# Linear attention ahead of two expert layers: a new order in the first rounds, and work moved in the last ones

## The chip, the cores and the metric

One core of one Trainium2 chip. The metric is the device time in microseconds (us) of one execution of the program. The kernel before took 772.84 us (median of 3 runs, 772.15 to 774.85).

## What is computed

Three layers, one behind the other, all in float32. The first is a linear attention with decay, over 4 batches, 8 heads, 768 steps and a head dimension of 48:

```python
for t in range(S):
    cur = einsum('bhd,bhe->bhde', u * k[t], v[t])
    y[t] = einsum('bhd,bhde->bhe', r[t], state + cur)
    state = w * state + einsum('bhd,bhe->bhde', k[t], v[t])
```

Its 3072 rows of 384 values go through a mixture of 8 experts (each token through the one with the largest logit, `relu(x @ w1[e]) @ w2[e]`, scaled by its gate) and then through a dense layer, `h = x @ w_in; (h - tanh(h)) @ w_out`.

## The kernel before, in words

**Tiles and rounds.** The sequence is cut into 6 chunks of 128 steps (C = 6); a tile is one chunk of one batch (B = 4), so there are 24 tiles, `seq[n]`, and the loop at L755 runs one round n for each, plus one more. Within a tile the recurrence is written as matrix products: the decays become tables of powers of w (`tables`, L284), with which r and k are scaled; the scores of all pairs of steps are masked to earlier ones, the diagonal holds the term with u, and the product with v gives the output. What earlier chunks left comes in through a state for each batch. Two buffers of scores (PSUM tags A0 and A1, one for the even and one for the odd heads) serve all tiles.

**The operations of a round**, by the engine that they run on:
- SP issues the loads, all from one queue in the order of the program: `load(n + 3)` (L233) brings n (r, k, v by token, 576 KB) and t (r, k transposed, 384 KB) of a tile into one of 5 buffers; `xout_g` writes finished rows to `xd`; `w_load` (L66) brings expert weights.
- POOL (GpSimd) computes `side`: rk = r*k, rku = rk*u, and `side_kh` (L349): kh = k*KT, for tile n + 2. `sw` (in `state_add`) scales the old state.
- DVE (VectorE): `diag_sum` (L354, dt) sums rku by head; `scale` (L324) multiplies r and k of tile n + 1 by the tables, k from round 3 on by PRK, a copy in SBUF; `mask` (L375) copies the scores of earlier steps into am; `state_add` (L393). Later rounds add the gate (`gate`), the ranks of the tokens (`rank_of`, `rank_in`), `head_end` (L492) and the subtraction of `w_split` (L79), which cuts a float32 weight in two parts.
- ACT (ScalarE): `diag` (L359) writes the 8 diagonals into am, one operation for each head; the copies of the output to y; xs (in `xout_g`, L573); the first half of `w_split`.
- PE (TensorE): `scores` (L366), `outp` (L408; the part on the old state is L418, the part with am L423), `state_mm` (L381, L390), `logits` (L447, L452), `xout_t` (L562; transposes of the output for `xout_g`). `keep_warm` (L586) issues products that nobody reads.

**Order.** Each engine works through its instructions in the order in which the program issues them; this block is scheduled by hand (`manual_schedule`), so the order of the calls is the order on each engine. Across engines semaphores order what depends on each other, buffers included. In round n the calls stand as: `load(n+3)`, `diag_sum(n+1)`, `scale(n+1)`, `logits`, `xout_t` (in rounds 5, 9, 13, ... it stands behind outp), `outp(n-1)`, `state_mm(n)`, `xout_g`, `diag(n+1)`, `scores(n)`, a second `xout_t` and `xout_g` where a round has two, `mask(n)`, `state_add(n)`, `side(n+2)`, `side_kh(n+2)`, and the gate and rank steps of a chunk that is complete. XOUT (L754) says which tiles leave in which of the last rounds; in the others it is tile n - 7. LOADS (L751) and SPLITS (L752) say in which round a half of a weight block is loaded and a quarter of it split.

**One PSUM bank.** `x_bank` (L433) hands the bank with tag X to `logits` and to `xout_t` in turn; from round 23 on a second one, K, takes every other turn:

```python
def x_bank(name):
    turns.append(name)
    tag = "K" if "both" in st and len(turns) % 2 else "X"
    return ps1.tile([P, HP, P], F32, tag=tag, name=name)
```

**Round 0 and the ends.** Ahead of the loop `in_range` (L267) tests the decays (each must lie between 3/4 and 4/3; for one that does not, a slow path runs, by the flag of `range_flag`, L279) and puts 1 in place of those that fail. In round 0 `k_rows` (L309) transposes the table of k on PE and copies it to KT on ACT, which kh needs. `gate_rows` (L247, round 0) clears pkg on DVE and loads the gate's columns in two transfers on SP's queue; `gate_cols` (L260, round 1) lays them out on POOL. Behind round 22's rank steps `head_gather` (L597) fetches, by index, the first rows of the first expert from `xd`, for which it needs idxh (an end of `idx_mm` in round 21) and the rows of tiles 0 to 15. After the loop PE transposes them (L610), and the experts' products and then the dense layer follow.

## Time and profile before

| | us |
|---|---|
| median of 3 runs | 772.84 |
| lowest, highest | 772.15, 774.85 |
| the profiled execution, its own time | 772.78 |
| its span, first to last instruction | 771.1 |
| PE busy | 755.7 (98% of the span) |
| DVE busy | 639.2 (83%) |
| ACT busy | 509.1 (66%) |
| POOL busy | 430.9 (56%) |

The profile is of one execution. Times of its rows count from the start of the span. Attention lies in the first 120 us or so, the experts up to about 375, the dense layer behind. "L372" is a line of the kernel before. PE is the engine of the matrix products, DVE VectorE, ACT ScalarE, POOL GpSimd, SP the queue that issues most transfers. "Idle before" is the time that an engine stood still ahead of an instruction, and the name behind the arrow is what ended it. The mean granted TensorE clock over the span was 0.996 of full speed.

### The profile page before, as it was taken

Reading aid. Unit: us, or ns where it says so; the run is one execution under the profiler, and the core shown is the slowest. Engines: PE = TensorE matmul, PEld = TensorE weight load, DVE = VectorE, ACT = ScalarE, POOL = GpSimd, SP = SyncE. Lnnn points to the kernel's source line nnn. Section 1 sums busy time; section 2 is a strip of 40 time slices with the busy share of each in tenths; the row PEclk is TensorE's granted clock in tenths of the full one; section 3 lists DMA queues with packets and bytes.
Section 4 is the critical chain, followed back from the end, with each engine's and each line's share of the span. In section 5 each row is a group of like instructions: output and inputs, shape, how many; then the busy total and the mean of one; then the engine's idle time right before and its main releaser. Section 6 shows DMA issues by size and latency. Waiting matters only on the chain.

```text
span 771.1 us, 14624 instructions
## 1 busy us (share of the span) xinstructions
PE 755.7 (98%) x5200; PEld 684.6 (89%) x5200; DVE 639.2 (83%) x1155; ACT 509.1 (66%) x1091; POOL 430.9 (56%) x435
## 2 busy tenths in 40 slices
PE   8899989999999999999999999999999999999997
PEld 7688868998999999999898998989989989899887
DVE  7899996788899888964898888888888888888893
ACT  6788885464454445554887766776777677677881
POOL 6989952385877876765355353443534344343433
PEclk9999999999999999999999999999999999999999
DMA  8999945466999899974000010000001000000101
GB/s 238 261 291 290 318 128 167 145 189 201 256 230 271 223 305 286 250 198 144 1 1 0 1 42 1 0 21 21 1 1 42 1 1 24 18 1 1 41 1 42
DMA packets 34656, 89.67 MB, mean 116 GB/s; under 512 B 5499, under 2 KB 12704, under 8 KB 34578
## 3 DMA queue, kind: packets, MB, share of 16 engines
q1 hardware_dynamic: 30384, 78.68, 34.8%
q0 software_dynamic: 4192, 9.99, 4.6%
q8 instruction: 43, 0.70, 0.4%
q14 instruction: 35, 0.29, 0.1%
q10 hardware_dynamic: 2, 0.00, 0.0%
HBM read 72.92 MB, written 15.74 MB: 115 GB/s over the span
## 4 chain that ended last, share of the span: by engine, by line
PE 51%; issue 2%; ACT 1%; POOL 1%; POOLq 0%
PE h L1346 25%; PE o L1394 24%; PE y L1119 1%; PE hps L1094 1%; POOL out_dram L1407 0%; PE o L1346 0%; POOL g L1383 0%; POOLq L1453 0%; POOL xb L1383 0%; ACT s L1354 0%; ACT mk L1356 0%; POOLq L1507 0%; ACT xb L1382 0%; ACT z L1350 0%; ACT t L1352 0%
## 5 line engine op out<-in xcount | busy, mean ns | idle before, releaser
L1383 POOL TENSOR_TENSOR g<-t,g 128x512 fp32r<-128x512 f32 x93 | 120.3, 1294 | 178.6 <-ACT g L1382 128.5
L1346 PE MATMUL h<-xb,ring 128*128 128x512 f32 x855 | 213.6, 395 | 0.0
L1394 PE MATMUL o<-ring,g 128*128 128x384 f32 x1116 | 209.3, 336 | 0.0
L1394 PEld LDWEIGHTS o<-ring,g 128*128 128x128 f32 x1116 | 196.1, 188 | 8.2
L1346 PEld LDWEIGHTS h<-xb,ring 128*128 128x128 f32 x855 | 159.7, 188 | 30.5
L85 POOL TENSOR_TENSOR ring<-stg,ring 128x384 fp32r<-128x384 f32 x102 | 105.3, 1053 | 53.8 <-ACT ring L84 42.4
L1350 ACT ACTIVATE z<-h 128x512 f32<-128x512 f32 x95 | 56.9, 599 | 95.2 <-PE h L1346 95.2
L1119 PE MATMUL y<-h,ring 128*128 128x256 f32 (+7 forms) x576 | 114.2, 342 | 0.6 <-DVE h L1098 0.6
L1094 PE MATMUL hps<-xt,ring 128*128 128x472 f32 (+6 forms) x504 | 105.6, 353 | 0.1
L1119 PEld LDWEIGHTS y<-h,ring 128*128 128x128 f32 x576 | 101.3, 188 | 4.1 <-DVE h L1098 1.0
L1362 DVE TENSOR_TENSOR t<-t,h 128x512 f32<-128x512 f32 x95 | 65.1, 685 | 41.3 <-ACT t L1352 40.9
L1094 PEld LDWEIGHTS hps<-xt,ring 128*128 128x128 f32 x504 | 90.6, 188 | 3.7 <-DVEq L1233 0.4
L1367 DVE COPY_PREDICATED t<-mk,h 128x512 f32<-128x512 uint32 x95 | 71.4, 751 | 10.1 <-DVE h L1365 0.5
L84 ACT CAST ring<-stg 128x384 fp32r<-128x384 f32 x152 | 70.2, 512 | 9.5 <-DMA stg<-in_wp_dram 8.9
L1364 DVE SCALAR_TENSOR_TENSOR h<-s,h 128x512 f32<-128x512 f32 x95 | 66.2, 697 | 10.6 <-ACT g L1382 0.9
L1097 ACT ACTIVATE h<-hps 128x256 fp32r<-128x256 f32 (+7 forms) x64 | 32.1, 501 | 63.8 <-PE hps L1094 61.8
L1354 ACT ACTIVATE s<-z,gb 128x512 f32<-128x512 f32 x96 | 69.6, 725 | 0.0
L1356 ACT ACTIVATE mk<-z,gt 128x512 f32<-128x512 f32 x96 | 69.3, 721 | 0.0
L1365 DVE SCALAR_TENSOR_TENSOR h<-z,h 128x512 f32<-128x512 f32 x95 | 66.1, 696 | 3.3
L1363 DVE TENSOR_TENSOR h<-h,z 128x512 f32<-128x512 f32 x95 | 65.9, 693 | 0.0
L1382 ACT CAST g<-t 128x512 fp32r<-128x512 f32 x93 | 57.6, 619 | 9.7 <-DVE t L1367 7.8
L363 ACT ACTIVATE am<-ident,dt 128x128 f32<-128x128 f32 x192 | 58.6, 392 | 3.8 <-DVE dt L356 3.8
(254 smaller groups left out, 1039.6 us busy)
## 6 DMA issues: line engine op xcount, KB each, us to landing
stg<-in_wp_dram SPq DMA_DIRECT2D x64, 384.0 KB, 4.9
n<-in_rkv_dram SPq DMA_DIRECT2D x24, 576.0 KB, 6.0
d<-in_wp_dram SPq DMA_DIRECT2D x32, 384.0 KB, 5.8
t<-in_rk_t_dram SPq DMA_DIRECT2D x24, 384.0 KB, 7.1
wdec<-dcf SPq DMA_DIRECT2D x32, 192.0 KB, 5.3
xd<-xs SPq DMA_DIRECT2D x24, 192.0 KB, 3.9
stg<-wdec SPq DMA_DIRECT2D x12, 384.0 KB, 4.3
wl<-wdec SPq DMA_DIRECT2D x2, 768.0 KB, 6.0
```

The lines of the kernel that those rows point to most:

```text
L84: nc.scalar.copy(out=dst[:, 0, sl], in_=of)
L85: eng.tensor_tensor(out=dst[:, 1, sl], in0=of, in1=dst[:, 0, sl].bitcast(F32), op=ALU.subtract)
L1094: nc.tensor.matmul(ps, lhsT=wf(a, kk), rhs=xt[e][b][:, kk, :], start=(n == 0), stop=(n == 8))
L1119: nc.tensor.matmul(yps[d], lhsT=wf(a)[:, d * P:(d + 1) * P], rhs=h2[:, b, :], start=(f == 0 and n == 0), stop=(f == CH1 - 1 and n == 2))
L1346: nc.tensor.matmul(ps, lhsT=wf(a, kk), rhs=xb[j][:, b, kk, :], start=(n == 0), stop=(n == 8))
L1354: nc.scalar.activation(out=s, in_=z, func=ACTF.Square, scale=G_K ** 0.5, bias=gb)
L1356: nc.scalar.activation(out=mk, in_=z, func=ACTF.Relu, scale=-1.0, bias=gt2)
L1364: nc.vector.scalar_tensor_tensor(out=ps, in0=s, scalar=G_K * G_D, in1=ps, op0=ALU.add, op1=ALU.mult)
L1365: nc.vector.scalar_tensor_tensor(out=ps, in0=z, scalar=G_A, in1=ps, op0=ALU.subtract, op1=ALU.mult)
L1367: nc.vector.copy_predicated(out=t, mask=mk.bitcast(U32), data=ps)
L1383: nc.gpsimd.tensor_tensor(out=g[:, 1, :], in0=ww, in1=g[:, 0, :].bitcast(F32), op=ALU.subtract)
L1394: nc.tensor.matmul(ops[q], lhsT=gg[i][:, b, q * P:(q + 1) * P], rhs=wf(a), start=(f == 0 and n == 0), stop=(f == CH2 - 1 and n == 2))
```

## The change

Seven edits. (1) The decays are bounded to 3/4 and 4/3 by one operation straight into the table of powers, and whether any was changed is found out in round 1 (`unchanged`). (2) keep_warm(14) ahead of the loop becomes keep_warm(8). (3) Round 0 begins with tile 0's scores, k_rows, the KT copy, the second half of its diagonals, its mask and its kh, ahead of diag_sum(1) and scale(1). (4) In rounds 1 to 4 scores(n), mask(n) and five of the eight diagonals of tile n + 1 stand ahead of outp(n-1); outp is cut in two functions for that, the part on the old state and the rest. (5) side_kh does nothing for the tiles of the last chunk (20 to 23), whose state nobody uses. (6) Tiles 12 to 15 leave two by two in rounds 19 and 20 in place of one each in 19 and 20 and two in 21; splits and one load move by a round or two, and two of the splits subtract on POOL in place of DVE. (7) head_end moves from round 19 to round 21, gate_cols from round 1 to round 3.

```diff
--- before.py
+++ after.py
@@ -199,7 +199,6 @@
     orow = ap_.tile([1, P], F32, name="orow")
     pkg = ap_.tile([P, 2, E * HP], F32, name="pkg")
     wcol, ucol = pkt[:, 0:HP], pkt[:, HP:2 * HP]
-    wsafe = ap_.tile([PT, HP], F32, name="wsafe")
     flag = ap_.tile([1, 1], I32, name="flag")
     wgp = ap_.tile([P, HP, 32], F32, name="wgp")
     sel = ap_.tile([P, E], F32, name="sel")
@@ -265,15 +264,13 @@
                                   in_=pkg[rows].rearrange("p q (i g e) -> p g q i e", g=2, e=E)[:, g])
 
     def in_range():
-
-        sq = ap_.tile([PT, HP], F32, name="sq")
-        nc.vector.tensor_mul(out=sq, in0=wcol, in1=wcol)
-        hi = ap_.tile([PT, HP], F32, name="hi")
-        nc.vector.tensor_single_scalar(out=hi, in_=sq, scalar=16.0 / 9.0, op=ALU.is_le)
+        nc.vector.memset(pw[:, :, 0:1], 1.0)
+        nc.vector.tensor_scalar(out=pw[:, :, 1:2], in0=wcol.unsqueeze(2), scalar1=0.75, scalar2=4.0 / 3.0,
+                                op0=ALU.max, op1=ALU.min)
+
+    def unchanged():
         ok = ap_.tile([PT, HP], F32, name="ok")
-        nc.vector.scalar_tensor_tensor(out=ok, in0=sq, scalar=9.0 / 16.0, in1=hi, op0=ALU.is_ge, op1=ALU.mult)
-        nc.vector.memset(wsafe, 1.0)
-        nc.vector.copy_predicated(out=wsafe, mask=ok.bitcast(U32), data=wcol)
+        nc.vector.tensor_tensor(out=ok, in0=wcol.unsqueeze(2), in1=pw[:, :, 1:2], op=ALU.is_equal)
         return ok
 
     def range_flag(ok):
@@ -283,9 +280,10 @@
 
     def tables():
 
-        for t, base, n in ((pw, wsafe.unsqueeze(2), 16), (pq, pw[:, :, 16:17], 8)):
-            nc.vector.memset(t[:, :, 0:1], 1.0)
-            nc.vector.tensor_copy(out=t[:, :, 1:2], in_=base)
+        for t, base, n in ((pw, None, 16), (pq, pw[:, :, 16:17], 8)):
+            if base is not None:
+                nc.vector.memset(t[:, :, 0:1], 1.0)
+                nc.vector.tensor_copy(out=t[:, :, 1:2], in_=base)
             m = 1
             while m < n:
                 nc.vector.tensor_tensor(out=t[:, :, m + 1:2 * m + 1], in0=t[:, :, 1:m + 1],
@@ -310,6 +308,10 @@
         kps = sm[:, 64:64 + HP * PT].rearrange("p (j t) -> p j t", t=PT)
         for j in range(HP):
             nc.tensor.transpose(kps[:, j, :], KD3[:, j, :], ident[0:PT, 0:PT])
+        st["kps"] = kps
+
+    def k_rows_end():
+        kps = st.pop("kps")
         nc.scalar.copy(out=KT.rearrange("p (j q) d -> p j (q d)", q=2), in_=kps[:, :, R0:R0 + 2 * D])
 
     def zero_pad(i, eng):
@@ -347,6 +349,8 @@
         side_rku(n)
 
     def side_kh(n):
+        if seq[n][0] == C - 1:
+            return
         kh = kh_b[n % 3]
         nc.gpsimd.tensor_tensor(out=kh[:, R0:].rearrange("p (h d) -> p h d", d=D), in0=n_b[n % NB][:, 1], in1=KT, op=ALU.mult)
         st["kh", n] = kh
@@ -356,12 +360,13 @@
         nc.vector.tensor_reduce(out=dt, in_=st.pop(("rku", n)), axis=AX.X, op=ALU.add)
         st["dt", n] = dt
 
-    def diag(n):
-        dt = st.pop(("dt", n))
-        am = at3.tile([P, 2, HP, P], F32, tag="am", name="am")
-        for h in range(H):
-            nc.scalar.activation(out=am[:, h % 2, h // 2, :], in_=ident, func=ACTF.Copy, scale=dt[:, h:h + 1])
-        st["am", n] = am
+    def diag(n, part=range(H)):
+        if 0 in part:
+            st["am", n] = at3.tile([P, 2, HP, P], F32, tag="am", name="am")
+        dt, am = st["dt", n], st["am", n]
+        for q, j in (divmod(k, HP) for k in part):
+            h = 2 * j + q
+            nc.scalar.activation(out=am[:, q, j, :], in_=ident, func=ACTF.Copy, scale=dt[:, h:h + 1])
 
     def scores(n):
         t = t_b[n % NB]
@@ -405,10 +410,8 @@
         state_mm(n)
         state_add(n)
 
-    def outp(n):
+    def outp_state(n):
         c, b = seq[n]
-        am = st.pop(("am", n))
-
         if c > 0:
             for i in range(2):
                 for g in range(2):
@@ -417,6 +420,10 @@
                         j, p0 = 2 * i + g, 64 * g
                         nc.tensor.matmul(Yp[q][p0:p0 + D, i, :], lhsT=Sc[c % 2][b][rows, j, :],
                                          rhs=t_b[n % NB][rows, 0, j, :], start=(i == 0), stop=False)
+
+    def outp(n):
+        c, b = seq[n]
+        am = st.pop(("am", n))
         for q in range(2):
             for j in range(HP):
                 i, p0 = j // 2, 64 * (j % 2)
@@ -724,12 +731,12 @@
         zero_pad(1, nc.scalar)
         keep_warm(6)
         u_rows()
-        keep_warm(14)
+        keep_warm(8)
         for i in range(3, NB):
             zero_pad(i, nc.scalar)
         consts()
         side_rk(0)
-        ok = in_range()
+        in_range()
         tables()
         NN = len(seq)
 
@@ -742,16 +749,16 @@
         side_rku(0)
         scale(0)
         diag_sum(0)
-        diag(0)
+        diag(0, range(HP))
         k_table()
         side(1)
         nc.gpsimd.memset(cum[0], 0.0)
-        LAG = 7
+        LAG, AHEAD = 7, B + 1
         L = C - 1
-        LOADS = {5: (0, 0), 9: (0, 1), 13: (1, 0), 15: (1, 1), 17: (2, 0), 20: (2, 1), NN - 1: (3, 0)}
-        SPLITS = {8: (0, 0), 12: (0, 1), 16: (0, 2), 18: (0, 3), **{NN - 3 + k: (1, k) for k in range(3)}}
+        LOADS = {5: (0, 0), 9: (0, 1), 13: (1, 0), 15: (1, 1), 17: (2, 0), 21: (2, 1), NN - 1: (3, 0)}
+        SPLITS = {9: (0, 0), 13: (0, 1), 17: (0, 2), 20: (0, 3, nc.gpsimd), 21: (1, 0, nc.gpsimd), 22: (1, 1), 23: (1, 2)}
         LATER = {0: ((3, 0), (3, 1)), 1: ((2, 2), (2, 3)), 2: ((3, 2), (3, 3))}
-        XOUT = {NN - 3: (NN - 10, NN - 9), NN - 2: (), NN - 1: (NN - 8, NN - 7), NN: ()}
+        XOUT = {NN - 5: (NN - 12, NN - 11), NN - 4: (NN - 10, NN - 9), NN - 3: (), NN - 2: (), NN - 1: (NN - 8, NN - 7), NN: ()}
         for n in range(NN + 1):
             if n == NN:
                 w_split(1, 3)
@@ -761,6 +768,13 @@
                 load(n + 3)
             if n in LOADS:
                 w_load(*LOADS[n])
+            if n == 0:
+                scores(0)
+                k_rows()
+                k_rows_end()
+                diag(0, range(HP, H))
+                mask(0)
+                side_kh(0)
             if n + 1 < NN:
                 diag_sum(n + 1)
                 scale(n + 1)
@@ -772,7 +786,13 @@
                 st["both"] = True
             if xs_of and not with_logits:
                 xout_t(xs_of[0])
-            if 1 <= n <= NN:
+            if n:
+                outp_state(n - 1)
+            if 0 < n < AHEAD:
+                scores(n)
+                mask(n)
+                diag(n + 1, range(5))
+            if n:
                 outp(n - 1)
                 at_step(n, 6, rank_row)
             if n > 1 and n < NN:
@@ -782,15 +802,16 @@
             if xs_of:
                 xout_g(xs_of[0])
             if 0 < n < NN - 1:
-                diag(n + 1)
+                diag(n + 1, range(5 if n < AHEAD else 0, H))
             if n < NN:
-                scores(n)
+                if n >= AHEAD:
+                    scores(n)
                 for m in xs_of[1:]:
                     xout_t(m)
                     xout_g(m)
-                mask(n)
+                if n >= AHEAD:
+                    mask(n)
                 if n == 0:
-                    k_rows()
                     diag(1)
                 elif n == 1:
                     state(0)
@@ -800,7 +821,6 @@
             if n + 2 < NN:
                 side(n + 2)
                 if n == 0:
-                    side_kh(0)
                     side_kh(1)
                 side_kh(n + 2)
             at_step(n, 3, logits2)
@@ -811,7 +831,7 @@
             at_step(n, 4, rank_mm)
             at_step(n, 4, rank_of)
             at_step(n, 5, rank_in)
-            if n == H0 * B + 3:
+            if n == NN - 3:
                 head_end()
             if n == NN - 2:
                 head_gather()
@@ -820,10 +840,11 @@
                 gate_rows()
             if n == 1:
                 scale_rows()
-                gate_cols()
+                ok = unchanged()
                 nc.vector.tensor_reduce(out=nok, in_=ok, axis=AX.X, op=ALU.add)
                 nc.vector.memset(one, 1.0)
             if n == 3:
+                gate_cols()
                 range_flag(ok)
                 nc.vector.tensor_copy(out=e8p, in_=e8)
                 nc.vector.tensor_copy(out=thp, in_=thr)
```

## Rows read from the trace of the kernel before

**Rows 1.** Page, engines; then stretches: us, busy us by engine, PE clock, DMA share, GB/s

```profile
PE 755.7 (98%) x5200; PEld 684.6 (89%) x5200; DVE 639.2 (83%) x1155; ACT 509.1 (66%) x1091; POOL 430.9 (56%) x435
...
28.00:30.00 2.00, 2.00 (x31) 1.81 (x29) 1.93 (x10) 0.77 (x3) 2.00 (x3) 0.56 0.95 250
30.00:32.00 2.00, 2.00 (x23) 1.80 (x19) 0.87 (x2) 2.00 (x8) 1.92 (x3) 0.59 1.06 256
...
80.00:90.00 10.00, 9.87 (x180) 7.49 (x176) 9.86 (x23) 9.18 (x29) 8.71 (x10) 1.00 1.02 304
...
140.00:160.00 20.00, 20.00 (x170) 19.88 (x170) 15.03 (x45) 10.86 (x28) 11.52 (x11) 1.00 0.58 179
```

**Rows 2.** Waits of POOL, 0 to 30 us: total us, times, longest

```profile
POOL rk L336 <- DMA n<-in_rkv_dram: 4.7, 3, 1.8
```

**Rows 3.** Timeline, 2 to 16 us: start us, us, engine, line, operation, idle before

```profile
2.88 0.14 DVE L270 TENSOR_TENSOR sq<-pkt 112x4 f32<-112x4 f32 x1
...
3.88 0.81 DVE L291 TENSOR_TENSOR pw<-pw 112x4 f32<-112x4 f32 x4
...
5.96 5.86 PE L589 MATMUL yh<-ident 128*128 128x128 f32 x28
...
13.49 0.48 ACT L313 COPY KT<-sm 128x384 f32<-128x384 f32 x1 [1.45 <-PE sm L312]
13.50 1.34 DVE L377 COPY_PREDICATED am<-mlt,A 128x512 f32<-128x512 uint32 x2
...
14.92 0.81 SPq L250 DMA_DIRECT2D pkg<-in_pk_dram  x2
```

**Rows 4.** Timeline, rounds 1 to 4

```profile
21.88 0.47 POOL L264 COPY wgp<-pkg 64x32 f32<-64x32 f32 x2
...
27.86 1.71 PE L423 MATMUL yh<-am,n 128*48 128x128 f32 x16 [1.70 <-DVE am L377]
...
30.29 1.80 PE L372 MATMUL A<-t 64*128 64x128 f32 x16
...
32.19 1.36 DVE L377 COPY_PREDICATED am<-mlt,A 128x512 f32<-128x512 uint32 x2 [1.32 <-PE A L372]
```

**Rows 5.** Timeline, rounds 18 to 21

```profile
95.96 0.81 DVE L85 TENSOR_TENSOR ring<-stg,ring 128x384 fp32r<-128x384 f32 x1
96.17 0.59 ACT L577 ACTIVATE xs<-Xps,gt 128x384 f32<-128x384 f32 x1
...
97.27 2.45 ACT L363 ACTIVATE am<-ident,dt 128x128 f32<-128x128 f32 x8 [0.51 <-DVE dt L356]
...
97.75 1.40 DVE L328 TENSOR_TENSOR t<-t,PRK 112x512 f32<-112x512 f32 x1
...
101.42 0.59 ACT L577 ACTIVATE xs<-Xps,gt 128x384 f32<-128x384 f32 x1
...
102.12 1.06 PE L452 MATMUL lps<-y,wgp 128*32 128x512 f32 x8
...
103.12 0.65 PE L418 MATMUL yh<-t,Sc 64*48 64x128 f32 x16
103.49 0.69 DVE L328 TENSOR_TENSOR t<-t,PRK 112x512 f32<-112x512 f32 x1
...
104.86 1.26 PE L423 MATMUL yh<-am,n 128*48 128x128 f32 x16 [1.09 <-DVE am L377]
...
105.83 0.71 ACT L428 COPY y<-yh 128x256 f32<-128x256 f32 x2
...
106.64 1.16 PE L372 MATMUL A<-t 64*128 64x128 f32 x16
...
108.16 1.34 DVE L377 COPY_PREDICATED am<-mlt,A 128x512 f32<-128x512 uint32 x2
...
110.62 0.56 DVE L85 TENSOR_TENSOR ring<-stg,ring 128x384 fp32r<-128x384 f32 x1 [0.53 <-ACT ring L84]
```

**Rows 6.** Timeline, the transposes behind the loop

```profile
119.84 0.77 PE L610 MATMUL hp<-ident,n 128*128 128x128 f32 x5 [0.64 <-DMA n<-xd,idxh]
```

## The prediction

> **What bounds the kernel now.** First the busy times and the table of stretches [rows 1]. PE is busy for 755.7 of 771.1 us, and from 140 us on without a break (20.00 of the first 20), so whatever the first 120 us gain or lose moves the end by as much; nothing later hides it. In those 120 us, attention runs 24 rounds, one for each tile, and in the middle of them VectorE is the full engine: 9.86 of 10 us in 80 to 90, with POOL at 8.71, ACT at 9.18 and the DMA engines at a share of 1.02 [rows 1]. A middle round is thus set by DVE, with three others close behind. The first rounds are another case: POOL waits three times for a tile's rows, 4.7 us in all [rows 2], and DVE waits for POOL's products or for PE. I follow the timeline of both ends, because the edits lie there.
>
> **Start, before the loop.** The range test is seven small DVE operations, from 2.88 to the first table product at 3.88 [rows 3]; a memset and one operation with two bounds replace them, at about 0.3 us as priced by the 0.14 of the first one and the gaps between, so 0.7 us go. That brings the tables and the scaling of tile 0 forward by at most 0.7; the end feels none of it unless the order behind it keeps it. On PE keep_warm(14) took 5.86 us for 28 products [rows 3]; 8 instead of 14 end at 5.96 + 16 x 0.209 = 9.3, so scores(0) can start there and not behind all 28, at 11.8.
>
> **Round 0.** The new order is scores(0), k_rows, KT copy, second half of diag(0), mask(0), and only then dt(1) and scale(1). The KT copy (0.48) now stands on ACT ahead of the second half of diag(0). Scores of a tile take 1.16 us [rows 5] at full clock and up to twice that at half; I take the slow end, 9.3 to 11.4, since nothing shows the clock up before. k_rows and its hand-over then end at 12.1, the KT copy at 12.6, four diag operations (half of 2.45) at 13.8, and the second half of mask(0) (0.67) at 14.5. DVE stands idle for most of 12.2 to 13.8. Behind it dt(1) and scale(1), an estimate of 1.8 us (two products of 0.69 as in [rows 5] and a short sum), end at 16.2, where the old order had all of it done at 14.84 (13.50 + 1.34). So mask(0) is no longer in front of a free engine: round 0 comes out 1.3 us later on DVE. If scores(0) runs at full clock it is 0.5 later. The memset of pkg stands behind scale(1), and SP's queue holds load(4) behind the two pkg transfers: their issue moves from 14.92 to 16.2, and load(4) with it. Tile 4's rows come up to 1.3 us later; how much of that a full DMA queue hides no row shows, so 0 to 1.3, and I take 0.9, nearer the upper end, because load(4) is issued straight behind. What this delay costs is bounded by the slack that POOL had there, which was small.
>
> **Rounds 1 to 4.** Scores(n) and mask(n) now stand ahead of outp(n-1) on PE. In the old order mask(3) -> outp(3) -> state products -> scores(4) -> mask(4) was a loop, which left DVE waiting 1.32 us for PE at mask(4) [rows 4]; outp(3) took 1.71 and scores(4) 1.80 at that point, behind 1.70 us in which PE stood idle, with a mean granted clock of 0.56 and 0.59 in 28 to 32, so mostly at the lower of its two levels, 1.2 and not 2.4 GHz [rows 1, 4]. With scores first that wait goes, whatever the clock. Rounds 1 to 3 waited for POOL and DMA, not for PE, and keep their length; the 1.3 us of round 0 are absorbed there up to what tile 4's delay costs, 0.3 to 0.7. On POOL kh(0) fills the idle time ahead of tile 2's rows and costs nothing; gate_cols (two copies, 0.47 together, and a memset, an estimate of 0.8 [rows 4]) leaves round 1, where it was on POOL's full queue, and stands ahead of tile 6's products in round 4, where POOL is as full, so it only changes place. Sum: 1.32 gained, 0.5 lost to tile 4, 0.5 lost as dt(6) waits for POOL: **0.3 us** earlier. Ends: 1.3 earlier if load(4) costs nothing, 0.6 later if all 1.3 come through and a clock drop adds to it.
>
> **Rounds 5 to 17** keep their work; three splits move by one round on an engine that stays full. Zero.
>
> **Rounds 18 to 21 on DVE.** Two subtractions go to POOL: 0.81 at 95.96, and 0.56 with 0.53 of waiting at 110.62 [rows 5]. kh(20) to kh(23) go from POOL. In row 97.75 the multiplication by PRK took 1.40 beside a kh, and 0.69 at 103.49 with POOL idle [rows 5]; so about 0.5 to 0.7 goes there. Head_end (five small operations, an estimate of 1.0) moves to round 21. On DVE alone this is worth 1.8 to 2.3 us. The Trainium skill, SBUF — State Buffer, section "Who interferes with whom", says that a DVE operation with two SBUF inputs and a GpSimd one that reads SBUF exclude each other for the whole instruction. By that rule, which the pair 1.40 and 0.69 bears out, the two splits put on POOL could each block a multiplication by PRK for up to that 0.7 us, and the sum would be 0.7 later where DVE has no spare time. That sum, 773.9, lies within the likeliest case and changes no chance.
>
> **Rounds 19 to 21 on ACT and PE.** This takes the gain away. The transposed outputs go through one PSUM bank, X, until round 23: xout_t needs the ACT copy xs of the one before to be done, and so does logits(4). Now tiles 12 and 13 leave in round 19 and 14, 15 in round 20, and the second xs of a round stands on ACT behind diag. In round 20 xout_t(14) stands on PE ahead of outp(19). From [rows 5]: xs(12) ends at 96.8 (96.17 + 0.59); diag(20) 2.45, to 99.2; xs(13) to 99.7; xout_t(14), an estimate of 0.65 like the row of L418, and outp_state(19) 0.65, to 101.0; outp(19) 1.26, its two copies to y (0.71 for both) and xs(14) 0.59, all overlapping, to 102.9; diag(21) to 105.3; xs(15) to 105.8. Only then logits(4) (1.06; before at 102.12), outp_state(20) 0.65, outp(20) of which scores(21) waits 0.9, scores(21) 1.16: mask(21) can start at 109.6, against 108.16. **1.4 us later**, with what DVE saved spent waiting in rounds 20 and 21. From mask(21) to the end of split(1,0) the old order has 3.0 us (108.16 to 110.62 + 0.56); the new one has head_end in place of the split and its wait, 1.0 for 1.1. So mask(23) is 1.4 later too; I take 1.3, as ACT's overlaps may be a little better. Ends: 0.5 later and 2.0 later, from the same rows with every overlap taken or none.
>
> **Behind the loop.** head_gather needs tile 15's rows written, and its second half made PE wait 0.64 at 119.84 [rows 6]. The rows are now written a round earlier, but POOL has split(1,0) ahead of the gather and idxh comes 1.4 later, so the gather keeps about its time while outp(23) moves back, and the wait goes: 0.6. Sum: -0.3 + 1.3 - 0.6 = +0.4. The profiled execution took 772.78 us (span 771.1 and 1.7 around it), 0.06 below the median of 772.84; so 772.78 + 0.4 = **773.2**. About 0.3%, 2.3 us, is what a measurement can tell from no change.
>
> **Rivals.** (a) The late rounds stay bound by DVE: if ACT's second xs came ahead of diag in effect, or the chain is shorter than its rows add up to, the 2.3 us on DVE and the gather's 0.6 count, with the 0.3 of the first rounds: 772.78 - 3.2 = 769.6. For it speaks the full DVE of [rows 1]; against it the order on ACT and the one bank: logits(4) at 102.12 started right behind xs(13), 101.42 + 0.59 [rows 5]. Chance 0.24. (b) Slower: PE's clock falls in round 20 or 21. In my chain PE stands idle from 103.5 to 105.8, longer than the 1.70 us before the slow stretch [rows 4]; if the clock halves there, logits, outp and scores(21) run at half speed, as outp(3) did with 1.71, and up to 1.7 us come on top (the slow stretch of [rows 1] lost 2 x 0.44 + 2 x 0.41): 773.2 + 1.7 = 774.9, and with the chain at its long end, 0.7 more, 775.6. It decides from the point where that idle time lies ahead of logits(4). Chance 0.2. (c) The first rounds lose: tile 4's delay and a clock drop behind the idle time of round 1 (PE has nothing from 14 to 16.2) give 0.6 later in place of 0.3 earlier, 774.1. Chance 0.08. (d) Nothing reaches the end because the DMA engines, at a share near 1 throughout, set the pace of the first ten tiles: then 0.3 falls away, and the time is 773.5, within the likeliest case.
>
> **The numbers.** The likeliest case, (d) within it, has 0.48: 771.7 to 774.4. All of it, most of (b) and (c), counts as the same; of (b) and the unknown ends some 0.14 lies above 775.1; of (a) and the upper ends of the first rounds some 0.24 below 770.5. Range: 769.8 to 775.4.
>
> **What would show it.** Right: scores(0) at about 9.4; the halves of mask(0) apart, with a wait for ACT; pkg's transfers after 16; no wait for PE at mask(4); twenty kh; logits(4) waiting for xs (L577) with PE idle about 2 us, DVE waiting for A at mask(21); no DMA wait at the head's transposes. Wrong: DVE full through rounds 20 and 21 and mask(23) before 114, which is (a); a granted clock near 0.5 between 104 and 111, which is (b).

## The result and the profile after

The changed kernel takes 778.71 us (median of 6 runs, 777.11 to 780.45) against 773.00 for the kernel before in the same comparison: ratio 1.0059, 95% interval 1.0038 to 1.0080. It is slower, by 0.6%. That lies above the forecast of 773.2 and above the range, which ended at 775.4. The profiled execution took 777.11 us with a span of 775.4, against 772.78 and 771.1.

The whole difference is made before the head's first product (the first product of the first expert, behind the transposes of its gathered rows). That product starts at 123.28 us before and at 127.61 after (last row of the next fence); from there to the end of the span it is 647.8 us in both (771.05 - 123.28 and 775.39 - 127.61). So in these two executions the start of this one instruction stands for the kernel's time. How far behind the old kernel the new one is, round by round (start of mask(n) in the two timelines, one execution each):

| | mask(4) | mask(5) | mask(9) | mask(10) | mask(14) | mask(18) | mask(20) | mask(21) | mask(23) | head's first product |
|---|---|---|---|---|---|---|---|---|---|---|
| before | 32.2 | 36.3 | 53.8 | 57.6 | 75.3 | 93.0 | 104.1 | 108.2 | 116.1 | 123.3 |
| after | 30.3 | 36.2 | 53.4 | 59.4 | 78.8 | 97.7 | 107.7 | 114.1 | 121.4 | 127.6 |
| later by | -1.9 | -0.1 | -0.4 | 1.8 | 3.5 | 4.7 | 3.6 | 5.9 | 5.3 | 4.3 |

The timeline of the changed kernel, first rounds and the two ends of the head's transposes (start us, us, engine, line, operation, and in brackets the idle time before it with what ended it):

```profile
5.97 3.78 PE L596 MATMUL yh<-ident 128*128 128x128 f32 x16
...
9.68 1.54 PE L377 MATMUL A<-t 64*128 64x128 f32 x16
...
11.32 0.75 DVE L382 COPY_PREDICATED am<-mlt,A 128x512 f32<-128x512 uint32 x1 [1.51 <-PE A L377]
...
11.79 0.48 ACT L315 COPY KT<-sm 128x384 f32<-128x384 f32 x1 [1.49 <-PE sm L310]
...
13.48 0.73 DVE L382 COPY_PREDICATED am<-mlt,A 128x512 f32<-128x512 uint32 x1 [1.40 <-ACT am L369]
...
15.93 1.16 PE L377 MATMUL A<-t 64*128 64x128 f32 x16 [2.38 <-issue]
15.93 0.82 SPq L249 DMA_DIRECT2D pkg<-in_pk_dram  x2
...
30.26 1.34 DVE L382 COPY_PREDICATED am<-mlt,A 128x512 f32<-128x512 uint32 x2
...
123.89 0.84 PE L617 MATMUL hp<-ident,n 128*128 128x128 f32 x6
...
127.61 1.32 PE L646 MATMUL hp<-f,ring 128*128 128x256 f32 x9
```

These answer to [rows 3], the last row of [rows 4] and [rows 6], and they are close to what was forecast (what the first rounds are worth is another question, taken up with the experiments): scores(0) at 9.68, the second half of mask(0) 1.40 late behind its diagonals, pkg's transfers 1.0 later than in [rows 3], no wait for PE at mask(4), no wait for a DMA at the head's transposes.

What was not forecast is in rounds 9, 13 and 17. First round 8 of the kernel before, where the split's subtraction stood (L85 on DVE, its cast L84 on ACT):

```profile
50.17 0.50 ACT L84 CAST ring<-stg 128x384 fp32r<-128x384 f32 x1
...
50.64 0.40 POOL L537 TENSOR_TENSOR hv<-OH,ohh 128x128 f16<-128x128 f16 x1 [1.04 <-DVE ohh L527]
...
51.07 0.55 DVE L85 TENSOR_TENSOR ring<-stg,ring 128x384 fp32r<-128x384 f32 x1
...
51.12 0.76 POOL L541 TENSOR_TENSOR rh<-hv,tileid 128x128 f16<-128x128 f16 x1
```

The same view of the changed kernel, round 9:

```profile
54.27 1.00 POOL L355 TENSOR_TENSOR kh<-n,KT 128x384 f32<-128x384 f32 x1
...
55.01 0.50 ACT L84 CAST ring<-stg 128x384 fp32r<-128x384 f32 x1
55.24 0.51 POOL L406 TENSOR_TENSOR sw<-Sc,pq 112x192 f32<-112x192 f32 x1
...
55.54 1.59 DVE L85 TENSOR_TENSOR ring<-stg,ring 128x384 fp32r<-128x384 f32 x1 [0.48 <-ACT ring L84]
55.72 1.00 POOL L338 TENSOR_TENSOR rk<-n 128x384 f32<-128x384 f32 x1
...
57.06 0.54 DVE L360 TENSOR_REDUCE dt<-rku 128x8 f32<-128x384 f32 x1
...
57.63 2.45 ACT L369 ACTIVATE am<-ident,dt 128x128 f32<-128x128 f32 x8 [1.11 <-DVE dt L360]
```

The split's subtraction (L85) takes 1.59 us, and 1.80 and 1.84 in rounds 13 and 17. In rounds 8, 12 and 16 of the kernel before it took 0.55. It waits 0.48 us for ScalarE's cast, and meanwhile GpSimd starts sw, and then rk; the subtraction ends at 57.13, 0.4 us after rk (56.72). Behind it stand dt(11), the diagonals of tile 11 and the scaling.

The late rounds in the changed kernel:

```profile
103.61 0.56 ACT L584 ACTIVATE xs<-Xps,gt 128x384 f32<-128x384 f32 x1
...
104.22 0.66 PE L577 MATMUL Xps<-ident,y 128*128 128x128 f32 x4 [1.97 <-ACT xs L584]
...
107.66 1.33 DVE L382 COPY_PREDICATED am<-mlt,A 128x512 f32<-128x512 uint32 x2 [1.38 <-PE A L377]
...
110.22 1.06 PE L459 MATMUL lps<-y,wgp 128*32 128x512 f32 x8 [2.07 <-ACT xs L584]
...
110.64 1.01 POOL L85 TENSOR_TENSOR ring<-stg,ring 128x384 fp32r<-128x384 f32 x1 [6.27 <-ACT ring L84]
110.84 1.36 DVE L330 TENSOR_TENSOR t<-t,PRK 112x512 f32<-112x512 f32 x1
...
114.07 1.38 DVE L382 COPY_PREDICATED am<-mlt,A 128x512 f32<-128x512 uint32 x2 [1.87 <-PE A L377]
```

This is the chain through the X bank that the prediction drew: PE waits 1.97 us for xs, logits 2.07, DVE 1.38 and 1.87 for the scores. The granted clock stays at 1.00 here.

### The profile page after: what moved, and what is told of

Same layout as the page of the kernel before. It is cut to its first block, busy times and chain, and to the rows that moved or that the text cites. A ratio compares the mean times of both kernels' runs of the same rounds, so it can differ in the third digit from the quotient of the medians.

```text
span 775.4 us, 14586 instructions
## 1 busy us (share of the span) xinstructions
PE 755.1 (97%) x5188; PEld 683.8 (88%) x5188; DVE 641.9 (83%) x1149; ACT 509.4 (66%) x1091; POOL 429.0 (55%) x433
## 4 chain that ended last, share of the span: by engine, by line
PE 51%; issue 2%; ACT 1%; POOL 1%; POOLq 0%
PE h L1367 25%; PE o L1415 23%; PE y L1140 1%; PE hps L1115 1%; POOL out_dram L1428 0%; PE o L1367 0%; POOL g L1404 0%; POOLq L1474 0%; POOL xb L1404 0%; ACT mk L1377 0%; ACT s L1375 0%; POOLq L1528 0%; ACT xb L1403 0%; ACT z L1371 0%; ACT t L1373 0%
## 5 line engine op out<-in xcount | busy, mean ns | idle before, releaser
L85 POOL TENSOR_TENSOR ring<-stg,ring 128x384 fp32r<-128x384 f32 x104 | 107.8, 1060 | 61.3 <-ACT ring L84 48.8
L1140 PE MATMUL y<-h,ring 128*128 128x256 f32 (+7 forms) x576 | 114.1, 342 | 0.6 <-DVE h L1119 0.6
L84 ACT CAST ring<-stg 128x384 fp32r<-128x384 f32 x152 | 70.2, 512 | 10.7 <-DMA stg<-in_wp_dram 9.2
L1403 ACT CAST g<-t 128x512 fp32r<-128x512 f32 x93 | 57.6, 619 | 9.6 <-DVE t L1388 7.7
```

What stands on the lines that cost most here:

```text
L84: nc.scalar.copy(out=dst[:, 0, sl], in_=of)
L85: eng.tensor_tensor(out=dst[:, 1, sl], in0=of, in1=dst[:, 0, sl].bitcast(F32), op=ALU.subtract)
L1140: nc.tensor.matmul(yps[d], lhsT=wf(a)[:, d * P:(d + 1) * P], rhs=h2[:, b, :], start=(f == 0 and n == 0), stop=(f == CH1 - 1 and n == 2))
```

## The experiments

Each set of kernels that ran together had its own runs of the kernel before, so the ratios are compared and not the medians. An interval is about 0.25% to either side, and the difference of two ratios is a little less certain still; a part's price is therefore read from several pairs of kernels that differ in that part alone, and no single pair settles it. Each profile is of one execution.

**e1: the first three splits back.**

```
-        SPLITS = {9: (0, 0), 13: (0, 1), 17: (0, 2), 20: (0, 3, nc.gpsimd), 21: (1, 0, nc.gpsimd), 22: (1, 1), 23: (1, 2)}
+        SPLITS = {8: (0, 0), 12: (0, 1), 16: (0, 2), 20: (0, 3, nc.gpsimd), 21: (1, 0, nc.gpsimd), 22: (1, 1), 23: (1, 2)}
```

> The changed kernel with one part undone: the first three expert splits are back in rounds 8, 12 and 16 (the change has them in 9, 13 and 17). Theory A, the moved splits cost the time: in the profile of the changed kernel mask(10), mask(14) and mask(18) come 1.8, 3.5 and 4.7 us later than before, about 1.6 us for each moved split. Then this kernel has mask(18) within 0.5 us of 93.0 us and takes 4.5 us less than the changed kernel, ratio to the kernel before 1.000 (0.998 to 1.002). Theory B, the late rounds cost the time (the chain through the X bank, mask(21) 5.9 us later, would be as late without the moved splits): mask(18) near 93 us, but mask(21) still 113 us or later, ratio 1.004 or more.

775.20 us, ratio 1.0020 (0.9994 to 1.0045). mask(18) came at 93.2, as both theories had it, and the subtractions took 0.55. But mask(20) came at 106.6 and mask(21) at 112.1, 2.5 and 4.0 us later than before. So both theories have a part: 0.39% of the loss left with the splits, and a part stayed in the late rounds. There the profile shows more than a longer chain:

```profile
100.51 1.11 PE L577 MATMUL Xps<-ident,y 128*128 128x128 f32 x4 [2.01 <-ACT xs L584]
...
102.59 1.95 PE L430 MATMUL yh<-am,n 128*48 128x128 f32 x16
...
104.47 2.08 PE L377 MATMUL A<-t 64*128 64x128 f32 x16
...
106.64 1.34 DVE L382 COPY_PREDICATED am<-mlt,A 128x512 f32<-128x512 uint32 x2 [4.88 <-ACT am L369]
```

The scores took 2.08 us, where 1.16 is usual. The stretches of the same kernel say why (us, busy us of PE, PEld, DVE, ACT, POOL, then granted clock, DMA share, GB/s):

```profile
95.00:100.00 5.00, 3.50 (x69) 3.22 (x67) 4.79 (x18) 3.92 (x13) 2.23 (x2) 1.00 0.94 250
100.00:105.00 5.00, 4.49 (x40) 3.43 (x42) 1.77 (x4) 1.25 (x4) 2.44 (x2) 0.50 0.79 261
105.00:110.00 5.00, 4.00 (x46) 2.52 (x44) 3.32 (x8) 4.22 (x12) 1.29 (x2) 0.82 0.24 85
```

After 2.01 us in which PE waited for xs, the clock was 0.50 for five microseconds, its lower level (1.2 of 2.4 GHz). That is rival (b), which the changed kernel's own profile does not show.

**e2: the three moved splits alone**, on the kernel before.

```
-        SPLITS = {8: (0, 0), 12: (0, 1), 16: (0, 2), 18: (0, 3), **{NN - 3 + k: (1, k) for k in range(3)}}
+        SPLITS = {9: (0, 0), 13: (0, 1), 17: (0, 2), 18: (0, 3), **{NN - 3 + k: (1, k) for k in range(3)}}
```

> The kernel before with that one part alone: its splits of rounds 8, 12 and 16 moved to rounds 9, 13 and 17. Theory A: each costs about 1.6 us, mask(18) at 97.5 us, ratio to the kernel before 1.005 to 1.006. Theory B: the loss is there at mask(18), but the later rounds wait for something else and take it up, ratio 1.001 or less.

776.84 us, ratio 1.0027 (1.0002 to 1.0051). That lies between the two expectations. The subtractions took 1.53 to 1.60 behind waits of 1.6 us in all, and mask(18) came at 96.4, 3.4 later than before; but this execution had reached mask(9) at 50.4, 3.4 earlier than the profile before, so from there to mask(18) it loses 6.7. The part alone makes the old kernel slower, by 2.1 us (0.27% of 773), less than the profile loses on the way to mask(18).

**e3: the late rounds back** (order of the x rows, that is of the finished rows that leave by XOUT; fourth to seventh split, the expert load, the head's end), and **e4: that and the first three splits back**, so that only the first rounds, the decays and the missing kh stay changed.

```
-        SPLITS = {9: (0, 0), 13: (0, 1), 17: (0, 2), 20: (0, 3, nc.gpsimd), 21: (1, 0, nc.gpsimd), 22: (1, 1), 23: (1, 2)}
+        SPLITS = {9: (0, 0), 13: (0, 1), 17: (0, 2), 18: (0, 3), **{NN - 3 + k: (1, k) for k in range(3)}}
...
-        XOUT = {NN - 5: (NN - 12, NN - 11), NN - 4: (NN - 10, NN - 9), NN - 3: (), NN - 2: (), NN - 1: (NN - 8, NN - 7), NN: ()}
+        XOUT = {NN - 3: (NN - 10, NN - 9), NN - 2: (), NN - 1: (NN - 8, NN - 7), NN: ()}
...
-            if n == NN - 3:
+            if n == H0 * B + 3:
                 head_end()
```

and the load of LOADS in round 21 in 20 again. e4 has 8, 12 and 16 for 9, 13 and 17 besides.

> The changed kernel with the late rounds undone: the order in which the x rows leave, the fourth split (vector engine, round 18), the splits of the last three rounds, the expert load of round 20 and the head's end are as in the kernel before; the splits of rounds 9, 13 and 17, the first rounds and the missing kh stay changed. Theory A: still slower than the kernel before by 4 to 6 us, ratio 1.005 to 1.008, since the loss is made before round 18. Theory B: 4 us back, ratio 1.000 to 1.002.

> The changed kernel with both undone: only the order of the first rounds, the decays bounded in one operation and the missing kh of the last chunk remain. Both theories: within 0.15% of the kernel before, 0.3 us less by the masks (mask(8) comes at 48.6 us in the changed kernel, 48.7 before). If it stays slower by 0.3% or more, the first rounds are to blame, which neither theory says.

e3: 779.45 us, ratio 1.0070 (1.0044 to 1.0096), no gain from the old late rounds. e4: 773.99, ratio 1.0016 (0.9992 to 1.0041): the first rounds are worth nothing that shows. e3's profile held a surprise. Its subtractions took 0.56 to 0.63 us although they stand in rounds 9, 13 and 17, and mask(18) came at 94.5. Its round 13:

```profile
73.00 1.01 POOL L355 TENSOR_TENSOR kh<-n,KT 128x384 f32<-128x384 f32 x1
73.33 0.50 ACT L84 CAST ring<-stg 128x384 fp32r<-128x384 f32 x1
...
73.86 0.56 DVE L85 TENSOR_TENSOR ring<-stg,ring 128x384 fp32r<-128x384 f32 x1
73.97 0.83 POOL L406 TENSOR_TENSOR sw<-Sc,pq 112x192 f32<-112x192 f32 x1
```

The cast ends at 73.83, the subtraction starts before sw, and sw takes 0.83 in place of 0.51. So the same order of instructions gives either price; a few tenths of a microsecond on ScalarE decide. This one execution, the shortest of e3's six, lost elsewhere: the head's first transposes waited 2.15 us for the gathered rows.

**e5: the cast earlier.** Only the ScalarE half of the split moves, ahead of the round's diagonals (`cast=None` issues the cast alone, `cast=False` the subtraction alone).

```
+            if n in (9, 13, 17):
+                w_split(*SPLITS[n], cast=None)
             if 0 < n < NN - 1:
                 diag(n + 1, range(5 if n < AHEAD else 0, H))
...
-                w_split(*SPLITS[n])
+                w_split(*SPLITS[n], cast=n not in (9, 13, 17))
```

> The changed kernel with the ScalarE cast of the splits of rounds 9, 13 and 17 put ahead of that round's diagonals instead of behind them; the VectorE subtraction stays where the change has it. Theory A, now with its mechanism: in the changed kernel the subtraction waits 0.3 to 0.5 us for this cast, GpSimd's sw and rk start meanwhile, and the subtraction takes 1.6 to 1.8 us beside them where it took 0.55 in round 8; the order of arrival sets the price. Then without the wait the subtraction takes 0.55 to 0.65 us in all three rounds, mask(18) comes 3 us or more earlier than in the changed kernel (by 94.7), and the time falls by 3 to 4 us, ratio to the kernel before 1.000 to 1.003. Rival C, rounds 9, 13 and 17 have no room for the operation however it arrives: the subtraction still takes over 1.4 us, ratio 1.005 or more.

775.15 us, ratio 1.0027 (1.0007 to 1.0048). Round 9 of its timeline:

```profile
54.63 1.00 POOL L358 TENSOR_TENSOR kh<-n,KT 128x384 f32<-128x384 f32 x1
...
55.34 0.72 DVE L88 TENSOR_TENSOR ring<-stg,ring 128x384 fp32r<-128x384 f32 x1
...
55.60 0.83 POOL L409 TENSOR_TENSOR sw<-Sc,pq 112x192 f32<-112x192 f32 x1
...
56.39 1.02 POOL L341 TENSOR_TENSOR rk<-n 128x384 f32<-128x384 f32 x1
```

The subtraction is ready while kh still runs. It takes 0.72 (0.70 and 0.73 in rounds 13 and 17), a little over the 0.65 expected, and it is now sw that pays, 0.83 for 0.51. mask(18) came at 93.6, 4.1 us earlier than in the changed kernel. Rival C falls: the rounds had room for the operation.

**e6: one input.** In rounds 9, 13 and 17 (`one`) the subtraction gives way to an operation of the same size that reads one tile in SBUF. The kernel leaves out the true low parts of these three splits.

```
+        if one:
...
+                eng.tensor_reduce(out=dst[:, 1, sl], in_=dst[:, 0, sl].bitcast(F32).unsqueeze(2), axis=AX.X, op=ALU.add)
+        else:
+            eng.tensor_tensor(out=dst[:, 1, sl], in0=of, in1=dst[:, 0, sl].bitcast(F32), op=ALU.subtract)
...
-                w_split(*SPLITS[n])
+                w_split(*SPLITS[n], one=n in (9, 13, 17))
```

> The changed kernel with the VectorE subtraction of the splits of rounds 9, 13 and 17 replaced by an operation at the same place, behind the same cast, that reads one tile in SBUF and writes as much (a reduction over an axis of one element); those low parts are then copies of the high parts, not differences. The wait for the cast stays. Theory A: two inputs in SBUF are what GpSimd's work holds up, so this takes 0.6 us or less although it arrives as late; mask(18) by 95.5 us, ratio 1.001 to 1.003. Rival D, it is the arrival behind the cast alone or the write that is held up: still over 1.4 us each, ratio 1.005 or more.

775.47 us, ratio 1.0030 (1.0012 to 1.0048). Round 9:

```profile
54.84 0.50 ACT L84 CAST ring<-stg 128x384 fp32r<-128x384 f32 x1
...
55.30 0.52 POOL L410 TENSOR_TENSOR sw<-Sc,pq 112x192 f32<-112x192 f32 x1
55.38 0.55 DVE L87 TENSOR_REDUCE ring<-ring 128x384 fp32r<-128x384 f32 x1 [0.27 <-ACT ring L84]
...
55.81 1.02 POOL L342 TENSOR_TENSOR rk<-n 128x384 f32<-128x384 f32 x1
```

It waits for the cast as in the changed kernel, in this round it comes while sw runs, as there, and it takes 0.55 (in the other two rounds it comes beside a kh and takes 0.55 as well; the waits are 2.2 us in all). Rival D falls. The wait for the cast is cheap by itself; what costs is that a two-input operation which comes second waits for GpSimd.

e5 and e6 gave back 4.1 and 3.7 us at mask(18) but only 0.3% of the time. In both profiles the late rounds then took longer, with the clock at 0.55 and 0.69 from 100 to 105 us, as in e1; each of these two profiles is of the longest of its kernel's twelve executions, so they show the late rounds at their worst.

**e7: the x rows as before, the splits back, two splits still on GpSimd.** Edits: e1's, and e3's XOUT alone.

> The changed kernel with the first three splits back in rounds 8, 12 and 16 and the order in which the x rows leave as in the kernel before; the fourth and fifth splits stay on GpSimd in rounds 20 and 21. It takes the chain through the X bank out of the late rounds and keeps what they save on VectorE. If that chain is what the late rounds lose (Xps waits 2.0 us for xs, and with the first three splits back the TensorE clock fell to 0.50 between 100 and 105 us): clock 1.00 from 95 to 115 us, the head's first product by 122.5 us (123.28 before), ratio 0.998 to 1.000. Rival: GpSimd's subtraction waits 5 to 6 us for its cast and holds up the rk behind it, whatever the x rows do: ratio 1.002 or more.

771.32 us, ratio 0.9991 (0.9969 to 1.0013). The head's first product came at 121.37, the clock stayed at 1.00 from 95 to 125, and Xps waited 0.3 us for xs:

```profile
100.00:105.00 5.00, 4.37 (x64) 2.73 (x60) 4.63 (x13) 4.63 (x14) 2.21 (x3) 1.00 0.86 248
105.00:110.00 5.00, 4.72 (x76) 3.88 (x74) 4.63 (x13) 4.32 (x14) 3.86 (x5) 1.00 0.44 142
```

Against e1, whose only difference is the x rows, 0.29% less. The rival here falls: GpSimd's L85 waits 1.3 us for its cast, not 5 to 6.

**e8: the early cast and the late rounds as before** (e3 with e5's edit).

> The cast ahead of the diagonals as in e5, and the late rounds as in the kernel before (as in e3, whose profile had subtractions of 0.55 to 0.63 us but a wait of 2.3 us for the head's gathered rows, 776.4 us, and a median of 779.5). If the late subtractions cost e3 its median: within 0.2% of the kernel before. If the head's rows and the transfers around them did: 777 us or more again, with the head's first transposes waiting over 1.5 us for a DMA.

774.83 us, ratio 1.0024 (1.0001 to 1.0047): between the two expectations. 0.46% came back against e3, which speaks for the late subtractions as the cost in e3's median (its one profile had them early). But the head's transposes waited 1.6 us for a DMA again, and the head's first product came at 126.03 although from mask(5) to mask(23) every mask stood within 0.5 us of the kernel before. Why the gathered rows come later there, the runs leave open; e7's profile has no such wait.

**e9 and e10: the changed kernel with the x rows as before**, with the early cast (e9) and without (e10).

> The changed kernel with two orders mended: the casts of rounds 9, 13 and 17 ahead of the diagonals (as e5) and the x rows leaving as in the kernel before (as e7). If the late cast and the x rows are the whole loss, this is e7 over again although the splits stay in rounds 9, 13 and 17: subtractions of 0.55 to 0.75 us, clock 1.00 from 95 to 115 us, the head's first product by 122.5 us, ratio 0.998 to 1.001. If the moved splits still cost something of their own: 1.002 or more.

> The changed kernel with the x rows alone leaving as in the kernel before; the casts of rounds 9, 13 and 17 stay late. With late rounds that do not hold anything up, the three subtractions should cost all of what they cost at mask(18), 3.5 to 4.7 us: ratio 1.004 to 1.006 against e7. If the x rows were the larger part: 1.002 or less.

e9: 773.31 us, ratio 0.9987 (0.9958 to 1.0017). e10: 776.83, ratio 1.0024 (0.9995 to 1.0054). By the ratio e9 is e7 over again: moved splits cost nothing that shows once their cast is early (0.72 to 0.73 each). Its profiled execution came late at the head, 124.37 and not 122.5, since the transposes waited 2.2 us for the gathered rows, as in e8. e10's subtractions took 1.69 to 1.82. It lies 0.33% above e7, a little less than the 0.4 to 0.6% expected.

**e11: only the late splits on GpSimd**, on the kernel before; **e12: only the order of the x rows**, on the kernel before; **e13: both.**

```
     def side_kh(n):
+        if seq[n][0] == C - 1:
+            return
...
-        SPLITS = {8: (0, 0), 12: (0, 1), 16: (0, 2), 18: (0, 3), **{NN - 3 + k: (1, k) for k in range(3)}}
+        SPLITS = {8: (0, 0), 12: (0, 1), 16: (0, 2), 20: (0, 3, nc.gpsimd), 21: (1, 0, nc.gpsimd), 22: (1, 1), 23: (1, 2)}
...
-            if n == H0 * B + 3:
+            if n == NN - 3:
                 head_end()
```

These are e11's (with the load of LOADS in round 20 in 21). e12 has the XOUT of the change in place of the old one, e13 has both.

> The kernel before with only the fourth and fifth split on GpSimd in rounds 20 and 21, no kh in the last chunk, the expert load of round 20 in 21 and the head's end two rounds later (that is e7 without the first rounds and without the decays in one operation). If the first rounds are worth nothing, as e4 has it: the same as e7, ratio 0.997 to 1.000. If they carry e7: 1.001 or more.

> The kernel before with only the order in which the x rows leave as in the change. If this order is the late rounds' loss by itself: Xps waits over 1.5 us for xs near 100 to 105 us, mask(20) or mask(21) waits over 1.2 us for PE or ACT, ratio 1.002 to 1.005, more where the TensorE clock falls. If it needs the splits on GpSimd beside it: 1.000.

> e11 (the kernel before with the two splits on GpSimd, no kh in the last chunk, the head's end later) with the new order of the x rows added. If the order costs 0.3 to 0.4% wherever GpSimd holds the two splits: 0.3 to 0.4% above e11, ratio to the kernel before 1.000 to 1.001, with Xps waiting about 2 us for xs. If it cost that only in the changed kernel, with its other first rounds: as e11, 0.996 to 0.998.

e11: 771.41 us, ratio 0.9965 (0.9933 to 0.9996), the one version whose interval lies wholly below the kernel before, and 0.26% below e7, so the new first rounds do not carry e7. e12: 774.45, ratio 0.9993 (0.9964 to 1.0022): no cost that shows. e13: 774.02, ratio 0.9987 (0.9965 to 1.0008), 0.22% above e11, less than expected. e12's profile has the chain all the same:

```profile
98.54 0.66 PE L570 MATMUL Xps<-ident,y 128*128 128x128 f32 x4 [1.90 <-ACT xs L577]
...
103.55 1.33 DVE L377 COPY_PREDICATED am<-mlt,A 128x512 f32<-128x512 uint32 x2 [1.33 <-PE A L372]
...
111.23 1.35 DVE L377 COPY_PREDICATED am<-mlt,A 128x512 f32<-128x512 uint32 x2 [3.53 <-PE A L372]
```

**e14: e5 with the second xs of a round ahead of its diagonals.**

```
+            for m in xs_of[1:]:
+                xout_t(m)
+                xout_g(m)
...
             if 0 < n < NN - 1:
                 diag(n + 1, range(5 if n < AHEAD else 0, H))
...
-                for m in xs_of[1:]:
-                    xout_t(m)
-                    xout_g(m)
```

> e5 (the changed kernel with the early cast) with the second pair of transposes and xs of rounds 19, 20 and 23 put ahead of that round's diagonals and scores, so that no xs stands behind eight diagonals. If the place behind the diagonals is the reason: no wait over 1.2 us of Xps or lps for xs in the profile, clock 1.00 from 100 to 110 us, ratio 0.998 to 1.001 against 1.0027 for e5. If the x rows cost through their transfers or through the diagonals being late instead: 1.002 or more.

774.36 us, ratio 1.0007 (0.9983 to 1.0030), 0.20% below e5. The clock stayed at 1.00 from 95 to 125, and the longest wait for xs was 0.96 us:

```profile
103.32 0.66 PE L580 MATMUL Xps<-ident,y 128*128 128x128 f32 x4 [0.96 <-ACT xs L587]
```

So the place behind the diagonals carries part of the x rows' price, as the prediction's chain has it, and not clearly all.

**The account.** The ratios to the kernel before, as a table of three choices:

| splits of the first half | x rows as in the change, two splits on GpSimd | x rows as before, two splits on GpSimd | all late rounds as before |
|---|---|---|---|
| rounds 9, 13, 17, late cast | 1.0059 (the change) | 1.0024 (e10) | 1.0070 (e3) |
| rounds 9, 13, 17, early cast | 1.0027 (e5) | 0.9987 (e9) | 1.0024 (e8) |
| rounds 8, 12, 16 | 1.0020 (e1) | 0.9991 (e7) | 1.0016 (e4) |

Down the columns, the late cast costs 0.32 to 0.54% in six comparisons (which share their ratios) and 0.27% in e2, about 3 us. From the second column to the first, the x rows cost 0.29 to 0.40% (0.22% in e13), about 2.5 us. From the third to the second, GpSimd's two splits (and the head's end and one load, which moved with them) gain 0.25 to 0.46%, 0.35% with kh in e11, about 2.8 us. The step from the kernel before to e4, the first rounds with the missing kh, is 0.16%, by itself not to be told from nothing. From e4 by e3 and e10 to the change: 0.16 + 0.54 - 0.46 + 0.35 = 0.59%; such a walk through the table always ends at the change's ratio, and shows only what sizes the parts have along it.

**The first rounds.** They have more pairs than that one: with the new first rounds e7 lies 0.26% above e11, e1 0.33% above e13 and e3 0.43% above e2. No pair is beyond doubt, but all four say slower, by about 0.3% or 2 us (e4 and e3 lack the kh of the last chunk besides). The profiles go the same way. Granted clock and masks of the changed kernel (first line) and of e2, which has the old first rounds (the other four: two stretches, mask(4), mask(5)):

```profile
18.00:20.00 2.00, 1.53 (x24) 1.37 (x20) 1.13 (x3) 2.00 (x8) 1.92 (x3) 0.50 0.85 266
...
18.00:20.00 2.00, 1.76 (x48) 1.79 (x48) 1.21 (x6) 1.32 (x4) 1.88 (x5) 1.00 1.06 295
28.00:30.00 2.00, 2.00 (x34) 1.04 (x34) 2.00 (x3) 2.00 (x8) 1.92 (x3) 1.00 1.07 262
...
29.63 1.35 DVE L377 COPY_PREDICATED am<-mlt,A 128x512 f32<-128x512 uint32 x2
...
33.31 1.35 DVE L377 COPY_PREDICATED am<-mlt,A 128x512 f32<-128x512 uint32 x2 [0.44 <-PE A L372]
```

In all eleven profiles with the new first rounds PE stands idle for 2.4 us ahead of scores(1) (the row at 15.93 above), and the granted clock is then at its lower level, 0.50 or 0.51, in 16 to 18 or in 18 to 20 us. In the five with the old ones it is 1.00 from 12 to 24. mask(5) comes at 35.5 to 37.4 in the eleven, and at 33.0 to 33.8 in e2, e11, e12 and e13; the kernel before itself, at 36.3, is the one of the five whose clock fell later on, to 0.56 in 28 to 30. So the table of masks in the section on the result sets the change against an execution with unusually late first rounds. That the low clock in round 1 is what makes mask(5) late is not tested by any run.

## Why the prediction was wrong

**The step that failed** is one line: "Rounds 5 to 17 keep their work; three splits move by one round on an engine that stays full. Zero." The work is the same, but its price is not. An operation's duration was taken from the round in which it stood. In round 8 it came behind three other DVE operations of the rank steps, when the cast was done, and before GpSimd's rh, which had to make way (0.76; in e11, where it did not, 0.40). In round 9 one short copy stands in their place, DVE arrives while ScalarE still has the cast behind eight diagonals, and GpSimd is in the middle of sw with rk behind it. 0.55 becomes 1.59 to 1.84. mask(18) is 4.7 us late in the profile, about three times 2.08 - 0.55 (the wait with the subtraction, for the old price); about 3 us of it are left in the runs. No rival held this. e5 and e6 show the cause: with the cast early, or with one input in place of two, the operation takes 0.55 to 0.73 in the same rounds.

The prediction even had the rule, and applied it elsewhere. The Trainium skill, SBUF — State Buffer, section "Who interferes with whom", also says that the order of issue, not the shape, decides which engine is held up. The runs agree with it in both directions: 1.53 to 1.84 us for the DVE operation that comes during sw (the changed kernel, e2, e10), 0.72 for it and 0.83 in place of 0.51 for sw where DVE comes first (e5), and, for an operation with one input that comes second, 0.55 (e6). Where the prediction did use it, it held too: the multiplication by PRK at 110.84 took 1.36 beside GpSimd's L85.

**The first rounds were a second miss.** "Sum: 1.32 gained, 0.5 lost to tile 4, 0.5 lost as dt(6) waits for POOL: 0.3 us earlier" rests on a wait of 1.32 us and a clock of 0.56 and 0.59 that belong to the one execution profiled before; the other four profiles with the old first rounds reach mask(4) at 29.3 to 29.7 without that wait, and the changed kernel's 30.26 is no gain on them. By the four pairs of ratios the first rounds cost about 2 us. Against the profile before, mask(9) came 0.4 earlier for the forecast 0.3: that is luck.

**The other steps.** The start and round 0 came out as worked out: the first table product at 3.16 for 3.88, the second half of mask(0) within 0.3 us, pkg 1.0 later for 1.3 (two slips of addition, 11.4 for 11.6 as the slow end of scores(0) and 99.7 for 99.8 at xs(13), change nothing). mask(4) came 1.9 earlier, and of that 0.1 was left at mask(5), where the old order sets in again. Late rounds: the chain through the X bank was put at 1.4 us at mask(21); from mask(18) to mask(21) the changed kernel loses 5.9 - 4.7 = 1.2. Xps, logits and DVE wait where it was said. Behind the loop 5.3 - 4.3 = 1.0 us came back, for 0.6. With 4.7 in place of zero the sum would have been 777.9; the profiled execution took 777.11. That closeness holds for these two executions; in the runs the late cast is smaller, and the first rounds make up for it.

**The parts of the late rounds** were forecast at 1.3 lost less 0.6 behind the loop; in the runs they come out near nothing (-0.11, 0.03 and 0.04% by the rows of the table), as two parts that cancel: about 2.8 us gained by moving two splits off DVE, for the 1.8 to 2.3 that the prediction named, and about 2.5 lost by the order of the x rows.

**The rivals.** (b), a falling clock, was real though it is not in the changed kernel's profile: e1, e5, e6, e12 and e13 have a granted clock of 0.50 to 0.84 between 100 and 105 us, behind a wait for xs of 1.3 to 3.2 us; the changed kernel with 1.97 has 1.00. It does not need the new order of the x rows: e2 has 0.67 from 105 to 110, behind a wait of 1.94 for a mask. (a) was wrong for the change, yet e11 shows a gain like the one that it named. (c), a clock drop behind PE's idle time in round 1, is in every profile of the new first rounds; its 0.6 us was small beside the 2 us that the pairs give, though no pair alone proves them.

**What stays open.** Why only about 3 us of the 4.7 at mask(18) are left in the runs; which part of the first rounds costs; why the x rows cost 0.2 to 0.4% beside GpSimd's splits and nothing that shows alone (e12), though its profile has the same waits; and why the profiled executions of e3, e8 and e9 wait for the gathered rows.

## What to carry to other kernels

When an operation moves, its price has to be read again at its new place: what is it ready behind, which engine shares its memory path at that moment, and which of the two gets there first. A split of work over two engines should have its first half well ahead on the other engine; 0.3 to 0.5 us of waiting for a cast cost over a microsecond each time. And a change that bundles several orders is worth taking apart: here a gain of 0.35% (e11, 771.41 us) was hidden under losses of about the same size. Last, a wait or a low clock read from one profiled execution may be that execution's alone: the kernels that share its instructions up to that point are the test.

## What the runs showed of the hardware

The price of a two-input DVE operation beside GpSimd jumps; it doesn't grow with the delay. Started 0.03 us after its cast and ahead of sw it took 0.56 (e3, round 13); ready during sw it took 1.80 (the changed kernel, round 13), since GpSimd went from sw straight to rk and DVE ended only 0.41 us after rk. It is so in all nine late subtractions of the changed kernel, e2 and e10: each ends 0.40 to 0.42 us after rk, and wait and subtraction add up to 2.07 to 2.11 us, however long the wait. One that comes while a kh runs is let in right behind it: 0.70 to 0.73 in e5, 1.03 in round 8 of e11, each ending 0.41 to 0.43 us after that kh. Why GpSimd gives way behind kh and not behind sw, the runs leave open. e3 and the changed kernel have the same instructions up to round 17, so two executions of one order can differ by this alone. And the low clock came in some kernels after PE had waited 2.0 us in round 19 or 20 (e1), or 1.27 (e13), and not in another after 1.97 (the changed kernel): the length of one wait in these rows does not tell which.
